# Batch 0's q in rows of nine, the token weight cast and then turned, output rows dealt anew (attention followed by a token and channel MLP, one Trainium2 core)

## The chip, the cores and the metric

The kernel runs on one core of one Trainium2 chip. The core has five engines that run side by side: PE (TensorE, matmuls; its weight loads are listed apart as PEld), DVE (VectorE), ACT (ScalarE), POOL (GpSimd) and SP (SyncE, which here issues nearly all transfers). Sixteen DMA engines move data between the chip's memory and the core's SBUF. The metric is the time of one execution in microseconds of device time. Shown times are medians of several runs; the profile is one execution taken by the hardware profiler.

## What is computed

```python
# attention without softmax, 8 batches x 8 heads, 576 tokens, head width 64
kv  = einsum('bhsd,bhse->bhde', k, v)
out = einsum('bhsd,bhde->bhse', q, kv)
out = out / sqrt(mean(out*out, -1) + 1e-6) * g_norm      # then heads side by side: x[b, s, 512]
# MLP over tokens, then over channels
a1  = alpha1 * x + beta1
tok = einsum('ts,bsd->btd', w_tok, a1)                   # w_tok is 576 x 576
u   = x + lam * tok
a2  = alpha2 * u + beta2
y   = u + lam * (maximum(a2 @ w_ch1, 0) @ w_ch2)         # 512 -> 2048 -> 512
```

Everything comes in and goes out as float32.

## The kernel before, in words

A batch has 576 tokens. The kernel holds them as four chunks of 128 and a tail of 64 (chunk 4); two batches share the tail tiles, one in the lower 64 partitions and one in the upper. For each batch the stages are: k and v come in and `kv_product` (L695) or, for batch 1, L798 and L808 multiply them; q comes in, is split into a high and a low bf16 part (`split_q`, L650), and is turned so that channels lie on partitions, by PE for batch 1 (`qt_dma`, L673) and by transposing DMAs from batch 2 on (L659); q times kv and the norm (`qkv_groups`, L1019, L1102); the token product (`tok_groups`, L1168, L1197); u is turned by transposing DMAs into `a2t` (`ut_groups`, L1307); the first channel product into `ht` (`ch1_groups`, L1328, L1370); the second (`ch2_groups`, L1419), whose result is added to u by DVE (L1429) and stored by one DMA per chunk (L1432), or by two for the shared tail (L1436). The last chunk of the last batch is done in two column parts (L1400, L1406, L1409). Batch b's second channel product is mixed with the preparation of batches b+1 and b+2.

Batch 0 goes a way of its own in float32: `load_first` brings k and v in rows of nine (partition p of a head takes tokens 9p to 9p+8, so that a partition reads 2304 bytes in one piece), two heads above one another. q comes in as 128 partitions of four tokens each (L568) with the last 64 tokens as separate tails (L594), is turned by PE with an identity (`qt_first`, L730, L745) and multiplied in `qkv_first` (L929, L954). The token weight comes in as 128 partitions of four rows each (L1521) and 64 more rows (L1525), into memory that `ht` takes later. `wt_groups` turns it by PE in float32 (L1565, L1588); ACT and DVE copy the results to `wt` as bf16. L1610 makes its column sums, L1242 is batch 0's token product. While PE has nothing to do before the first channel product it runs filler matmuls on zeros (L1750).

Because a partition holds four neighbouring tokens, chunk c holds the tokens 4p + OFF[c] with OFF = (0, 2, 1, 3), and a store writes a chunk with one transfer of 128 rows:

```python
P.op("SP", 0.6, lambda e: e.dma_start(out[b, OFF[c]:512:4, :], x), r=keys, dma_us=0.8)
```

The order is not written out by hand. Each operation is recorded with an engine (or a choice of engines), a cost, what it reads (`r`) and writes (`w`); `Prog.plan` and `Prog.schedule` lay the operations out in time by these costs, by due times and by a table of hand-set shifts of single operations at the end of the kernel, and each engine then runs its own list in that fixed order. All transfers but six small ones go out from SP in its list's order; batch 1's k and v wait for "gate", which the second `kv_product` of batch 0 sets.

Of the kernel before, what the change touches and what calls it, by code (L numbers as in the profile page):

```python
# [6 lines left out]
F32 = mybir.dt.float32  # L7
# [456 lines left out]
def bass_transnormer_attn__then__resmlp_affine_kernel(  # L464
# [15 lines left out]
    with ExitStack() as stack:  # L480
# [18 lines left out]
        qf = sb("qf", [128, NH, 4, DH], F32)  # L499
        qft = sb("qft", [128, NH, DH], F32)  # L500
# [5 lines left out]
        qt32 = qflat[:, 0:2048].rearrange("p (h c t) -> p h c t", h=NH, c=2)  # L506
        qtl32 = qflat[:, 2048:2304].rearrange("p (r t) -> p r t", r=4)
# [11 lines left out]
        a2t = sb("a2t", [128, 4, TP + 16], BF16)  # L519
# [7 lines left out]
        wst2 = hst[0:64, 2304:2880]  # L527

# [38 lines left out]
        def load_main(tile, key, src, b, hs, eng="SP"):  # L567
            P.op(eng, 0.6, lambda e: e.dma_start(  # L568
                tile[:, hs].rearrange("p h c d -> p h (c d)"),
                src[b, hs, 0:512, :].rearrange("h (p c) d -> p h (c d)", c=4)),  # L570
                w=[(key, a) for a in range(hs.start // 4, hs.stop // 4)],
                dma_us=3.7 if hs == ALL[0] else 1.5 if hs.start else 2.0)

        def load_tail(tile, key, src, b, lo, eng="SP"):
            P.op(eng, 0.6, lambda e: e.dma_start(
                tile[lo:lo + 64, :, :], src[b, :, 512:576, :].rearrange("h s d -> s h d")),
                w=[key] + [("qft0", a, y) for a in range(2) for y in range(2) if lo == 0],
                dma_us=0.75)
# [5 lines left out]
        def load_first(a):  # L584
            for key, src, tile in (("kf", k, kf), ("vf", v, vf)):
                P.op("SP", 0.6, lambda e, src=src, tile=tile: e.dma_start(
                    nine(tile, 0, a).rearrange("p x c d -> p x (c d)"),
                    src[0, 4 * a:4 * a + 4].rearrange("(x y) (p c) d -> (y p) x (c d)",
                                                      y=2, c=9)),
                    w=[(key, a)], dma_us=2.0 if a and key == "vf" else 1.4)  # L590

        def load_first_tail(a):
            for y in range(2):
                P.op("SP", 0.45, lambda e, y=y: e.dma_start(  # L594
                    qft[0:64, 4 * a + 2 * y:4 * a + 2 * y + 2, :],
                    q[0, 4 * a + y:4 * a + y + 3:2, 512:576, :].rearrange("h s d -> s h d")),
                    w=[("qft0", a, y)], dma_us=0.2)
# [20 lines left out]
        def load_q(b, hs=ALL[0], tails=True):  # L618
            load_main(qf, "qf", q, b, hs)
            if tails:  # L620
                load_tail(qft, "qft%d" % (b % 2), q, b, 64 * (b % 2))

        PAIRS = ((0, 1), (2, 3), (4,))
        OFF = (0, 2, 1, 3)
# [4 lines left out]
        def split_q(b):  # L629
# [4 lines left out]
            for cs, hs in parts:  # L634
# [4 lines left out]
                if n == 1:  # L639
                    src, hi, lo = qft[rows, hs], hi[:, 0], lo[:, 0]  # L640
                    kin = ["qft%d" % par]
                else:
                    src = qf[:, hs, c0 // 2:c0 // 2 + 3:2, :].rearrange("p h c d -> p c h d")
                    kin = [("qf", a) for a in aa]
# [75 lines left out]
        def qt_first():  # L720

            def pair(a, j):
                t = P.ptile(1)
                h0 = 4 * a + 2 * j

                def f(e):
                    for h in range(2):
                        for c in range(2):
                            o = 256 * h + 128 * c
                            m = e.transpose(t.flat()[:, o:o + 128],  # L730
                                            qf[:, h0 + h, 2 * c:2 * c + 2, :].rearrange(
                                                "p c d -> p (c d)"), ident[:])
                    return m
                P.op("PE", 0.5, f, ins=8, r=["ident", ("qf", a)], w=[t])
                P.op(act_dve(512), 0, lambda e: copy(
                    e, qt32[:, h0:h0 + 2].rearrange("p h c t -> p (h c t)"), t.flat()),
                    r=[t], w=[("q32", 2 * a + j)])

            def tail(a):
# [9 lines left out]
                P.op("PE", 0.14, f, ins=4, r=["ident"] + [("qft0", a, y) for y in range(2)], w=[t])  # L749
                P.op(act_dve(128), 0, lambda e: copy(  # L750
                    e, qtl32[:, 2 * a:2 * a + 2, :],
                    t.flat()[:, 0:128].rearrange("p (r s) -> p r s", r=2)),
                    r=[t], w=[("q32t", a)])
            for a in range(2):
                yield lambda a=a: pair(a, 0)
                yield lambda a=a: pair(a, 1)
                yield lambda a=a: tail(a)
# [85 lines left out]
        def xv(b, cs, lo=0, hi=DM):  # L843
# [6 lines left out]
            return xm[rows, b % 2, cs[0]:cs[0] + len(cs), lo:hi]  # L850

        def rv(b, cs, lo=0, hi=DM):
# [5 lines left out]
            return rt[rows, b % 2, cs[0]:cs[0] + len(cs), lo:hi]  # L858
# [11 lines left out]
        def qkv_first():  # L870
# [48 lines left out]
            def main(a):  # L919
                ts = [P.ptile(1), P.ptile(1)]  # L920

                def f(e, j):
                    for c in range(2):
                        for h in range(2 * j, 2 * j + 2):
                            for sh in range(2):
                                for x in range(2):
                                    kr = slice(64 * x, 64 * x + 64)
                                    o = 256 * c + 64 * h
                                    mm = e.matmul(  # L929
                                        ts[x].flat(slice(64 * sh, 64 * sh + 64))[:, o:o + 64],  # L930
                                        qt32[kr, 4 * a + h, c, 64 * sh:64 * sh + 64],
                                        kv32[kr, a, (h + 2 * x) % 4, :], start=True, stop=True,
# [6 lines left out]
                for x in range(2):  # L939
                    norm(lambda x=x: ts[x].flat().rearrange("p (c h d) -> p c h d", c=2, h=4),  # L940
                         (2 * x, 2 * x + 1), HALVES[a], ts[x])

            def tail(a):
# [4 lines left out]
                hs = HALVES[a]  # L948

                def f(e):  # L950
                    for j in range(2):
                        for x in range(2):
                            kr = slice(64 * x, 64 * x + 64)
                            mm = e.matmul(t.flat(kr)[:, 64 * j:64 * j + 64],  # L954
                                          qtl32[kr, 2 * a + j, :], kv32[kr, a, j, :],
                                          start=True, stop=True, skip_group_check=True)
                    return mm
                P.op("PE", 0.2, f, ins=16, r=QT + KVD + [("kv32", a, 0), ("q32t", a)], w=[t])
                sqv, smv = sq4[:, sqs, 0:128], small[:, sms, 0:2]
                P.op("ACT", act_us(128), lambda e: e.activation(  # L960
                    sqv, t.flat()[:, 0:128], ACT.Square), r=[t], w=[("sqh", sqs)])
                P.op("DVE", dve_us(128), lambda e: e.tensor_reduce(
                    out=smv, in_=sqv.rearrange("p (h d) -> p h d", h=2), axis=AX.X, op=ALU.add),
# [6 lines left out]
                lo, hi = 256 * a, 256 * a + 256  # L970
                xk, rk = xkeys(0, 4, hs), rkeys(0, 4, hs)
# [821 lines left out]
```

## Time and profile before

| | |
|---|---|
| Median of 3 runs | 356.81 us (356.22 to 357.19) |
| The profiled execution | 356.91 us |
| Its span, first to last instruction | 355.1 us |
| Granted PE clock over the span | 1.000 |
| Read from memory, written to it | 38.82 MB, 9.44 MB |

A profile page gives each engine's busy time as a share of the span, a strip of 40 equal slices with the busy tenths of each, the transfers, and the chain of work that ended last. "PE busy" counts pipelined matmuls, so that a busy PE is not one at its peak. L with a number is a line of the kernel above. In the strip 9 means a busy share of at least 90%; for DMA it is the mean of all 16 DMA engines, so that one engine more loaded than the others doesn't show in it.

### The profile page before, as it was taken

What the parts mean: (1) busy time and instruction counts of PE and PEld (TensorE: products, weight loads), DVE (VectorE), ACT (ScalarE), POOL (GpSimd) and SP (SyncE); (2) the same over time, 40 slices, a digit from 0 to 9 for tenths busy, and PEclk for the clock granted to TensorE, in tenths of its full rate; (3) what the DMA queues carried; (4) which work ended last, traced back from release to release, by engine and by line L of the source; (5) the groups of instructions that cost most, each with busy time, mean ns of one, the idle gap of its engine ahead of it and who ended that gap; (6) DMA issues with size and microseconds to landing.
All of it is one profiled execution on the core that took longest, in us unless ns stands there. A gap on an engine that the chain in (4) does not pass through costs nothing.

```text
span 355.1 us, 7785 instructions
## 1 busy us (share of the span) xinstructions
PE 344.1 (97%) x3501; PEld 198.9 (56%) x3320; DVE 238.7 (67%) x365; ACT 157.0 (44%) x267; POOL 22.2 (6%) x30
## 2 busy tenths in 40 slices
PE   7998999999999999999999999999999999999996
PEld 6776644567554554467644654457744554457643
DVE  3679997874889579968883389945974378830021
ACT  3646961248722585038720386018620285007600
POOL 4161123300000000000000000000000000000000
PEclk9999999999999999999999999999999999999999
DMA  8999999999983599269704496244404010150022
GB/s 280 337 360 372 394 346 362 252 203 248 294 231 78 152 379 154 64 198 346 136 18 133 157 319 133 46 148 64 89 4 146 33 30 2 30 153 11 0 61 89
DMA packets 82761, 60.83 MB, mean 171 GB/s; under 512 B 55773, under 2 KB 66277, under 8 KB 82728
## 3 DMA queue, kind: packets, MB, share of 16 engines
q1 hardware_dynamic: 82704, 60.32, 58.7%
q8 instruction: 27, 0.44, 0.6%
q14 instruction: 6, 0.05, 0.0%
q10 hardware_dynamic: 24, 0.01, 0.0%
HBM read 38.82 MB, written 9.44 MB: 136 GB/s over the span
## 4 chain that ended last, share of the span: by engine, by line
PE 88%; DVE 6%; DMA 3%; issue 1%; SPq 0%
PE ps L1419 30%; PE ps L1370 18%; PE ps L1328 14%; PE ps L1168 7%; PE ps L695 4%; PE ps L1019 2%; PE ps L458 2%; PE ps L1197 1%; DMA vf<-in_v_dram 1%; DVE xm L1429 1%; DMA qt<-qs 1%; DVE a2b L1185 1%; DVE xm L1181 1%; PE ps L1400 1%; PE ps L1217 1%
## 5 line engine op out<-in xcount | busy, mean ns | idle before, releaser
L1419 PE MATMUL ps<-w,ht 128*128 128x512 bf16 x537 | 122.5, 379 | 2.3 <-issue 1.4
L1317 ACT ACTIVATE ht<-ps,hb 128x640 bf16<-128x640 f32 (+1 forms) x112 | 83.7, 747 | 48.7 <-PE ps L1370 35.9
L1419 PEld LDWEIGHTS ps<-w,ht 128*128 128x128 bf16 x560 | 53.5, 98 | 63.6 <-issue 2.0
L1370 PE MATMUL ps<-a2t,w 128*128 128x320 bf16 (+1 forms) x512 | 72.2, 299 | 0.4 <-DMA a2t<-a2b 0.4
L1370 PEld LDWEIGHTS ps<-a2t,w 128*128 128x128 bf16 x512 | 49.5, 98 | 21.4 <-DMA a2t<-a2b 0.8
L1328 PE MATMUL ps<-a2t,w 128*128 128x512 bf16 x232 | 52.7, 379 | 1.3 <-issue 0.6
L766 ACT ACTIVATE kvd<-ps 64x128 bf16<-64x128 f32 x24 | 6.5, 271 | 85.4 <-PE ps L695 85.3
L1328 PEld LDWEIGHTS ps<-a2t,w 128*128 128x128 bf16 x240 | 22.6, 98 | 26.5 <-DMA a2t<-a2b 0.4
L1429 DVE TENSOR_TENSOR xm<-ps,xm 128x512 f32<-128x512 f32 x31 | 20.7, 688 | 24.8 <-PE ps L1419 24.5
L1168 PE MATMUL ps<-rt,wt 128*128 128x512 bf16 x106 | 25.2, 379 | 0.4 <-issue 0.2
L1041 DVE TENSOR_REDUCE small<-sq 128x16 f32<-128x1024 f32 x14 | 16.8, 1214 | 12.9 <-ACT sq L1039 12.7
L1181 DVE TENSOR_TENSOR xm<-ps,xm 128x1024 f32<-128x1024 f32 x14 | 17.1, 1222 | 8.0 <-PE ps L1217 5.1
L695 PEld LDWEIGHTS ps<-vf,kf 64*64 64x64 f32 x1008 | 16.0, 135 | 6.3 <-issue 4.5
L564 ACT ACTIVATE qs<-qf 128x1024 bf16<-128x1024 f32 x13 | 13.4, 1049 | 13.5 <-DMA qf<-in_q_dram 10.7
L1185 DVE TENSOR_TENSOR a2b<-xm,a_bc 128x512 bf16<-128x512 f32 x28 | 18.7, 709 | 0.5
L771 DVE TENSOR_TENSOR kvd<-ps,kvd 64x128 bf16<-64x128 f32 x24 | 6.9, 288 | 18.0 <-ACT kvd L766 17.6
L695 PE MATMUL ps<-vf,kf 64*64 64x64 f32 x1008 | 17.9, 221 | 0.6 <-DMA vf<-in_v_dram 0.6
L1168 PEld LDWEIGHTS ps<-rt,wt 128*128 128x128 bf16 x112 | 10.9, 98 | 12.9 <-issue 0.4
L650 DVE TENSOR_TENSOR qs<-qf,qs 128x1024 bf16<-128x1024 f32 x14 | 16.9, 1217 | 1.5 <-ACT qs L564 1.5
L1060 DVE TENSOR_TENSOR xm<-ps,small 128x1024 f32<-128x1024 f32 x14 | 17.1, 1221 | 0.4
L1429 DVE TENSOR_TENSOR xtl<-ps,xtl 128x512 f32<-128x512 f32 x4 | 2.8, 692 | 20.2 <-PE ps L1419 20.1
L1019 PEld LDWEIGHTS ps<-kvd,qt 128*128 128x128 bf16 x224 | 13.9, 98 | 2.5 <-DMA qt<-qs 0.6
(146 smaller groups left out, 327.9 us busy)
## 6 DMA issues: line engine op xcount, KB each, us to landing
out_dram<-xm SPq DMA_DIRECT2D x31, 256.0 KB, 2.5
qf<-in_q_dram SPq DMA_DIRECT2D x7, 1024.0 KB, 11.4
kf<-in_k_dram SPq DMA_DIRECT2D x6, 1152.0 KB, 7.4
vf<-in_v_dram SPq DMA_DIRECT2D x6, 1152.0 KB, 8.5
stg<-in_moe_w_ch_dram SPq DMA_DIRECT2D x3, 1024.0 KB, 14.1
kf<-in_moe_w_ch_dram SPq DMA_DIRECT2D x2, 1024.0 KB
kf<-in_k_dram SPq DMA_DIRECT2D x2, 576.0 KB, 4.8
vf<-in_v_dram SPq DMA_DIRECT2D x2, 576.0 KB, 5.6
```

The source lines that it names most:

```text
L650: lambda e, hi=hi, lo=lo, src=src: e.tensor_tensor(out=lo, in0=src, in1=hi, op=ALU.subtract), r=kin + kh, w=kl, port=True)
L695: m = e.matmul(t.ap(slice(64 * x, 64 * x + 64))[:, y, 0:64], nine(kf, b, a)[r, x, c, :], nine(vf, b, a)[r, x, c, :], start=(c == 0), stop= ...
L1019: e.matmul(o, w, kvd[:, h, 0, :], start=True, stop=False)
L1060: P.op("DVE", dve_us(64 * m), lambda e: e.tensor_tensor(out=x3, in0=split(raw()), in1=inv, op=ALU.mult), r=[t, ("sm", sms)], w=xk, pri=-200)
L1168: m = e.matmul(t.ap()[:, i, :], tok_w(sc, c), rsrc(b, sc), start=(sc == 0), stop=(sc == 4))
L1181: P.op("DVE", dve_us(512 * n), lambda e: e.tensor_tensor(out=x, in0=t.ap(rows) if n > 1 else t.flat(rows), in1=x, op=ALU.add), r=[t] + xk, ...
L1185: P.op("DVE", dve_sb(512), lambda e, c=c: e.tensor_tensor(out=a2b[rows, c, :], in0=xv(b, (c,)), in1=a2_bc[rows, :], op=ALU.mult), r=xkeys( ...
L1317: o = P.op("ACT", act_us(n) + 0.07 * (b > 0), lambda e: e.activation(dst, src(), ACT.Relu, bias=hb[:, fj:fj + 1]) if b else e.activation(d ...
L1328: m = e.matmul(t.flat(), w, a2t[:, dj, 0:512], start=(dj == 0), stop=(dj == 3))
L1370: m = e.matmul(t.ap()[:, i, 0:n], w1[:, dj, 128 * fj:128 * fj + 128], a2t[:, dj, 320 * i:320 * i + n], start=(dj == 0), stop=(dj == 3))
L1419: m = e.matmul(t.flat(), ht[:, fj, 128 * c:128 * c + 128], w2[:, fj, :], start=(fj == 0), stop=(fj == 15))
L1429: P.op("DVE", dve_us(512), lambda e: e.tensor_tensor(out=x, in0=t.flat(), in1=x, op=ALU.add), r=[t] + keys, w=keys)
```

## The change

Four parts. Batch 0's q is loaded like k and v, two transfers of 512 KB in rows of nine without tails. So that the chunks agree for all batches, chunk c now holds the tokens 9p+c and 9p+c+4 for p from 0 to 63, and the tail holds the tokens 9p+8; q of the later batches is loaded as two transfers for 64 partitions each plus the tail, the token weight as four transfers for 64 partitions each plus the tail, and the stores write rows of that order. The token weight is cast to bf16 first (five casts into memory that `w1` takes later) and turned by matmuls with a bf16 identity in pieces of 64 columns. The table of shifts is a new one. `a2t` is 48 columns wider.

```diff
-        a2t = sb("a2t", [128, 4, TP + 16], BF16)
+        a2t = sb("a2t", [128, 4, TP + 64], BF16)
...
+        wflat = w1[:].rearrange("p j f -> p (j f)")
+        wb = wflat[:, 0:2304].rearrange("p (c s) -> p c s", c=4)
+        wb2 = wflat[0:64, 2304:2880]
...
+        def rows_at(ap, lo, n):
+
+            return ap.rearrange("(p c) f -> p c f", c=9)[:, lo:lo + n, :]
...
+        def load_q0(a):
+            P.op("SP", 0.6, lambda e: e.dma_start(
+                q9[:, 2 * a:2 * a + 2].rearrange("p z c d -> p z (c d)"),
+                q[0, 4 * a:4 * a + 4].rearrange("(z y) (p c) d -> (y p) z (c d)", y=2, c=9)),
+                w=[("qf", a)], dma_us=1.4)
+
+        def load_q(b):
+            v = q[b].rearrange("h (p c) d -> p h c d", c=9)
+            for u in range(2):
+                P.op("SP", 0.6, lambda e, u=u: e.dma_start(
+                    qf[64 * u:64 * u + 64].rearrange("p h c d -> p h (c d)"),
+                    v[:, :, 4 * u:4 * u + 4, :].rearrange("p h c d -> p h (c d)")),
+                    w=[("qf", 0), ("qf", 1)] if u == 0 else ["qfu"], dma_us=1.85)
...
+        def rows_of9(ap, c):
+
+            return ap.rearrange("(p c) f -> c p f", c=9)[c:c + 5:4]
...
-                    for pr in range(2):
-                        h = 4 * a + 2 * pr
-                        m = e.transpose(t.flat()[:, 64 * pr:64 * pr + 64],
-                                        qft[0:64, h:h + 2, :].rearrange("p h d -> p (h d)"),
-                                        ident[0:64, 0:64])
+                    for a in range(2):
+                        for z in range(2):
+                            m = e.matmul(t.flat(slice(64 * z, 64 * z + 64))[
+                                :, 128 * a:128 * a + 128], q9[:, 2 * a + z, 8, :], ident[:],
+                                start=True, stop=True, skip_group_check=True)
...
-                        out[b, OFF[c]:512:4, cols], x[:, cols]), r=keys, dma_us=0.6 if n > 128 else 0.3)
+                        rows_of9(out[b], c)[:, :, cols], x[:, cols]), r=keys, dma_us=0.6 if n > 128 else 0.3)
...
-                    P.op("SP", 0.6, lambda e: e.dma_start(out[b, OFF[c]:512:4, :], x), r=keys,
+                    P.op("SP", 0.6, lambda e: e.dma_start(rows_of9(out[b], c), x), r=keys,
                          dma_us=0.8)
                 else:
                     for i in range(2):
                         P.op("SP", 0.6, lambda e, i=i: e.dma_start(
-                            out[b - 1 + i, 512:576, :], x[64 * i:64 * i + 64, :]),
+                            out[b - 1 + i, 8:S:9, :], x[64 * i:64 * i + 64, :]),
                             r=xkeys(b - 1 + i, c), dma_us=0.4)
...
+            for u in range(2):
+                P.op("SP", 0.6, lambda e, u=u: e.dma_start(
+                    wst[64 * u:64 * u + 64, 2 * i:2 * i + 2, :],
+                    rows_at(moe_w_tok, 4 * u + 2 * i, 2)),
+                    w=[("wst", i)] if u == 0 else [("wsu", i)], dma_us=0.8)
+
+        for what, i in (('k', 0), ('v', 0), ('q', 0), ('k', 1), ('v', 1), ('q', 1), ('w', 0), ('w', 1), ('w', 2)):
...
+            w = wb[:, tc, :] if tc < 4 else wb2
+            return [w[:, x:S:9] for x in ((sc, sc + 4) if sc < 4 else (8,))]
...
+            def cast(m):
+                src, dst = (wst[:, m, :], wb[:, m, :]) if m < 4 else (wst2, wb2)
+                P.op(act_dve(576, 1.7), 0, lambda e: copy(e, dst, src),
+                     r=[("wst", m // 2), ("wsu", m // 2)] if m < 4 else ["wst2"], w=[("wb", m)], port=True)
...
                         for x in range(2):
                             o = 256 * y + 128 * x
-                            m = e.transpose(t.flat(slice(0, n))[:, o:o + 128],
-                                            wrow(i + 2 * x, s0 + y), ident[:])
+                            for z, ap in enumerate(wrow(2 * i + x, s0 + y)):
+                                m = e.matmul(t.flat(slice(64 * z, 64 * z + 64))[:, o:o + 128],
+                                             ap, identb[:], start=True, stop=True,
+                                             skip_group_check=True)
```

The turning of the token weight is then 32 such matmuls in four groups, four for the last 64 columns and nine for its tail rows, 45 in all, where there were 25 transposes. The norm of batch 0's tail is done once for all eight heads instead of once for each half. The split of q (`split_q`) and the loops of `qkv_first` follow the new order of the chunks.

More of the change, by code (lines that the diff above doesn't have):

```diff
@@ L756, in qt_first @@
                 yield lambda a=a: pair(a, 1)
-                yield lambda a=a: tail(a)
+            yield tail
         def kv_nine(b):
@@ L1579, in both @@
+            yield last
             def both():
@@ L1684, in mark @@
                 due[o] = 78
+        for i in range(4):
+            for m in range(5):
+                P.readers.setdefault(("w1p", i, 0), []).extend(P.readers[("wb", m)])
         P.chain = True
@@ L1754, in bass_transnormer_attn__then__resmlp_affine_kernel @@
         P.plan(due, 8, {
[7 rows of a table removed]
-            154: "DVE", 181: "DVE", 182: "POOL", 211: "POOL", 215: "DVE"})
[7 rows of a table added]
+            47: "ACT", 58: "ACT", 88: "POOL", 146: "DVE", 168: "ACT", 211: "POOL"})
         P.synchronize()
```

244 lines of the change are left out of this document (119 added, 125 removed), and 14 rows, old and new, of the table start.

## The prediction

> **What bounds the kernel now.** I read the page first, then the DMA view of single stretches, then the chain and the timeline.
>
> ```profile
> span 355.1 us, 7785 instructions
> ...
> PE 344.1 (97%) x3501; PEld 198.9 (56%) x3320; DVE 238.7 (67%) x365; ACT 157.0 (44%) x267; POOL 22.2 (6%) x30
> ...
> DMA  8999999999983599269704496244404010150022
> ```
>
> PE runs from start to end: only 11 us of the span are without a matmul. So time is gained only where PE's own work gets shorter or where it waits or fills, and lost wherever something makes it wait. The DMA strip says what could: the first eleven slices are full, later ones half. The time outside the span is 356.91 - 355.1 = 1.8 us; the profiled execution lies 0.1 us above the median of 356.81, so sums against it are sums against the median.
>
> **Stores.** A chunk's store had 128 rows as the outer dimension on both sides. Now the memory side is 2 x 64 rows, and the 2 lies outermost; the SBUF side still has 128. What does that do? First the price of a store. One stands alone between 345 and 350 us; the DMA view of that stretch says:
>
> ```profile
> DMA packets 144, 0.26 MB, mean 52 GB/s; under 512 B 16, under 2 KB 16, under 8 KB 144
> ...
> q1 hardware_dynamic: 144, 0.26, 13.6%
> ...
> out_dram<-xm SPq DMA_DIRECT2D x2, 256.0 KB, 2.3
> ```
>
> 128 packets are the rows, and 16 small ones stand beside them: I read these as one closing write from each of 16 engines. The store's work is 0.136 x 5 us x 16 = 10.9 engine-us, 0.68 us when all 16 share it. Now transfers with few rows, the six on ACT's queue (four of one row, two of four rows: twelve rows): the queue's packets, first and last of the six:
>
> ```profile
> q10 hardware_dynamic: 24, 0.01, 0.0%
> ...
> xm<-in_moe_lam_dram ACTq DMA_DIRECT2D x1, 2.0 KB
> ...
> xtl<-in_moe_beta_dram ACTq DMA_DIRECT2D x1, 2.0 KB
> ```
>
> Twelve rows would give 12 + 6 x 16 = 108 packets if every transfer closed on 16 engines. There are 24: one closing write for each row. A transfer is thus dealt to engines along its outer dimension, one engine for one row, four for four. [...] No run of before has a large transfer with so small an outer dimension, so its cost is bounded: 0.68 us if it is spread nevertheless, 10.9 / 2 = 5.4 us on two engines. I take 5.4, as the ACT queue's rows are the nearest.
>
> [...]
>
> **What 5.4 us does at the end.** Timeline of SP, and the page's row of the last store (64 KB, 1.7 us to landing):
>
> ```profile
> 342.60 7.24 SPq L1432 DMA_DIRECT2D out_dram<-xm  x3
> 351.98 0.96 SPq L1409 DMA_DIRECT2D out_dram<-xm  x2
> ```
> ```profile
> out_dram<-xm SPq DMA_DIRECT2D x1, 64.0 KB, 1.7
> ```
>
> The last three chunks' stores are issued from 342.6 on, some 3.5 us apart, then the two parts of the last chunk (192 and 64 KB, by bytes 4.1 and 1.4 us on two engines). They no longer keep up: they queue, and end at 342.6 + 1.6 + 3 x 5.4 + 4.1 + 1.4 = 365.9, where 1.6 is a store's landing time less its transfer (2.3 in the 345 to 350 stretch, less 0.68). Before, the last landed at about 352.6 + 1.7 = 354.3. **Plus 11.6 us**, and no work can hide it, since nothing follows.
>
> **What it does in the body.** DMA view of 72.5 to 232.5 us (first store to the transposes of batch 5's a2t), and of 232.5 to 342.5:
>
> ```profile
> q1 hardware_dynamic: 50880, 28.97, 68.2%
> ...
> qf<-in_q_dram SPq DMA_DIRECT2D x5, 1024.0 KB, 11.4
> ...
> out_dram<-xm SPq DMA_DIRECT2D x16, 256.0 KB, 2.5
> ...
> a2t<-a2b SPq DMA_TRANSPOSE x19, 2.4
> ```
> ```profile
> q1 hardware_dynamic: 12768, 6.29, 22.5%
> ...
> out_dram<-xm SPq DMA_DIRECT2D x12, 256.0 KB, 2.7
> ```
>
> In the first stretch an engine has 0.682 x 160 = 109.1 us of work, 16 x 0.68 = 10.9 of it stores. The two store engines would have 109.1 - 10.9 + 16 x 5.4 = 184.6 us in 160: 24.6 us too much. To this comes the next term.
>
> **Loads in halves.** q of the later batches now goes to 64 partitions at a time. The trace has such transfers: the tail's store is two of 64 rows. DMA view of 339 to 342.5, and then two stretches of the early loads, 13 to 14 (128 partitions) and 15 to 16 us (by SP's order, the token weight's 64 last rows pass about there):
>
> ```profile
> DMA packets 160, 0.26 MB, mean 75 GB/s; under 512 B 32, under 2 KB 32, under 8 KB 160
> ...
> q1 hardware_dynamic: 160, 0.26, 32.3%
> ```
> ```profile
> 13.00:14.00 1.00, 1.00 (x72) 1.00 (x71) 0.97 (x4) 0.71 (x3) 0.00 (x0) 1.00 0.99 392
> ...
> 15.00:16.00 1.00, 0.85 (x6) 0.50 (x5) 0.94 (x4) 1.00 (x3) 0.88 (x1) 1.00 0.96 180
> ```
>
> All 16 engines take part (32 closing writes for two), yet the same 256 KB cost 0.323 x 3.5 x 16 = 18.1 engine-us against 10.9, 1.66 times as much; and from 15 to 16 us the engines are busy (0.96) while only 180 GB/s move instead of 392. So half the partitions take bytes at about half the rate. Bounds for 1 MB of q: 4 x 0.68 = 2.7 us if halves cost nothing, 5.4 at half the rate; I take 1.66 x 2.7 = 4.5, plus 1.8 us for each of five loads, 9 us.
>
> [...]
>
> So the two engines are 24.6 + 9 = 33.6 us behind where batch 5's transposes go out. Timeline of SP and PE:
>
> ```profile
> 225.19 7.33 SPq L1307 DMA_TRANSPOSE a2t<-a2b  x5
> 236.96 2.34 PE L1370 MATMUL ps<-a2t,w 128*128 128x320 bf16 x16
> ```
>
> They left SP by 232.5, landed 2.4 us later, and PE took them at 236.96: 2.1 us of slack. The transposes stand in the same queue behind the stores, so PE would **wait some 31 us** in all up to there, spread over the batches. What else is queued: SP issues in order, so that q, k and v of the next batch and the transposes of q stand behind the stores too, but those have tens of microseconds of slack. After 232.5 an engine has 0.225 x 110 = 24.8 us, the two 24.8 + 12 x 4.7 = 81 in 110: they catch up, and no more is lost before the end. Bounds of this term: 0 (the slack of other stages covers all) to 40.
>
> **The head.** The chain, before the first channel product:
>
> ```profile
> 11.91 1.03 PE ps L1750 x4
> ...
> 15.65 0.54 PE ps L1750 x2
> 16.19 0.95 PE ps L1565 x8
> ...
> 17.52 0.82 PE ps L1565 x6
> 18.34 0.68 PE ps L1588 x5
> 19.02 0.82 PE ps L1565 x6
> ...
> 25.29 2.02 PE ps L798 x64
> ...
> 34.72 1.07 PE ps L673 x16
> ```
>
> The token weight's transposes take 0.95 + 0.82 + 0.68 + 0.82 = 3.27 us of PE. New: 45 products, 128 columns each, at 1.07 / 16 = 67 ns in L673: 3.0 us one after another, half if the two 64-column halves run side by side as in L798 (32 ns for each 64 x 64 pass). Their weights are strided, which costs:
>
> ```profile
> L1565 PEld LDWEIGHTS ps<-ident,ht x20: 108/208/212, 15.8 to 19.4; 128*128 128x128 f32 x16, 128*64 128x64 f32 x4
> L730 PEld LDWEIGHTS ps<-ident,qf x16: 137/140/142, 8.2 to 14.8; 128*128 128x128 f32 x16
> ```
>
> 208 ns strided against 140; half of 208 for 64 columns, and none hidden, gives 45 x 0.104 = 4.7 us. So between -1.8 and +1.4 us; I take -1.4, since L1565 itself took 119 ns each in spite of its 208. The five casts (576 columns) stand on DVE or ACT; the nearest rows are casts of 1024, below them two stretches of the windows view:
>
> ```profile
> 27.80 0.68 DVE L565 CAST w<-ht 128x1024 bf16<-128x1024 f32 x1
> ```
> ```profile
> 29.57 1.06 ACT L564 ACTIVATE w<-ht 128x1024 bf16<-128x1024 f32 x1
> ```
> ```profile
> 15.00:20.00 5.00, 4.85 (x53) 3.96 (x55) 3.77 (x13) 3.67 (x11) 2.94 (x4) 1.00 1.04 296
> ...
> 45.00:50.00 5.00, 4.95 (x24) 2.19 (x24) 4.82 (x8) 4.15 (x8) 2.00 (x1) 1.00 1.04 366
> ```
>
> so 0.4 or 0.6 us each, 2 to 3 us in all where DVE and ACT together have 2.6 us free in five; the first stands on the path: +0.5. Without that cover it would be 3. On the other side the token weight's 1.18 MB come in halves: 3.0 us at 392 GB/s become 5.0 (times 1.66), bounds 0 to +3.5; the DMA engines are full until 50 us, so this delays k and v of batch 1 and all weights after them: **+2.0**. The q tails that go away save four issues on SP and as many bytes come in larger pieces; it helps k and v of the second half, where PE fills for 1.03 us: -0.4. Turning q costs PE what it did (the tail's products pass twice in float32). The norm of the tail, done once instead of twice, frees some DVE and ACT. Sum of the head: -1.4 + 0.5 + 2.0 - 0.4 = +0.7, from -3 to +4. DVE is 96% busy from 45 to 50 us, so that a gain on PE ahead of this does not come through whole. The new table of shifts can't put right what it doesn't model; I price it at nothing, within 1 us either way. The wider `a2t` moves addresses only: nothing, for lack of a row that says otherwise.
>
> **Sum.** 356.8 + 11.6 + 31 + 0.7 = **400 us**. In this case the range is 367 (the end alone, with the best head) to 412.
>
> **Rivals.**
> *Stores spread after all, the head gains.* If the two-part side is dealt over 16 engines like 128 rows, nothing is lost behind the head; halves that overlap take the +2.0 away: 356.8 - 1.4 + 0.5 - 0.4 - 0.4 (DVE) = 355.1. For it: only a four-row transfer shows the dealing, and that one had no more than four rows to deal. Faster.
> *Stores spread, halves eat it.* The head's sum then stands alone: 356.8 + 0.7 to + 4, say 359; it decides as soon as halves cost over 1.3 us. The 15 to 16 us row speaks for it.
> *Nothing moves.* Token weight and DMA are later by what PE saves: 356.8.
> *Only the end pays.* Two engines, but the slack of the body takes all: 356.8 + 11.6 = 368; it lies in the first case's range.
>
> **How the numbers follow.** Two engines: 0.62. Spread and faster: 0.20. Spread and about equal: 0.08. Spread and slower: 0.10. This kernel's measurement tells 0.3% (1.1 us) from no change. So faster 0.20, same 0.08, slower 0.72. The range must reach from the spread cases to the two engines: 354.6 to 412, leaving half of the faster case below and little above.
>
> **What would show it.** Right: landing of the xm stores far above 2.5 us; the lone store's 16 closing writes become two; a2t's landing grows from 2.4 us and PE waits on it at L1328 and L1370; ten or more microseconds between the last DVE add and the end. Wrong: 16 closing writes and 2.5 us. For the head: L1565's group near 1.9 us, GB/s near 200 while the token weight and q land, casts between 14 and 20 us. If the stores are spread, the time is 355 to 359 and my main term is nothing.

## The result, and the profile after

The changed kernel took 463.31 us (median of four runs), the kernel before 356.97 beside it: 1.297 times as long, interval 1.289 to 1.304. Forecast were 400 us, within 354.6 to 412. The sign and the main cause held, the size did not: 106 us instead of 43. One of the four runs (500.89 us), with the granted clock lowered throughout (0.73), is left out of the ratio, and since the first profile fell on that run, the profile below is of a repetition (median 461.89 us, the profiled execution 460.99).

The page of the repetition: span, busy times, and the strips of the granted clock and of the transfers.

```profile
span 459.2 us, 7860 instructions
...
PE 366.2 (80%) x3532; PEld 207.7 (45%) x3350; DVE 239.6 (52%) x363; ACT 158.2 (34%) x265; POOL 22.0 (5%) x29
...
PEclk9999999899997999885899958998789989999995
DMA  8999999956093939557058871295405720021111
```

PE was busy 97% of the span before and is now busy 80%. Its clock strip, all nines before, has gaps. The transfer strip ends in four ones, a busy share of one to two tenths: two of sixteen engines are 0.125, and PE has nothing to do in the last of these slices.

Where do 459.2 - 355.1 = 104.1 us come from? The windows view in stretches of 40 us, first of the kernel before (80 to 352 us), then of the changed one (80 to 440), columns as in the prediction:

```profile
sum 272.00, PE 268.60 PEld 149.91 DVE 175.76 ACT 115.95 POOL 0.00; mean PE 38.37 PEld 21.41 DVE 25.11 ACT 16.57 POOL 0.00
```
```profile
200.00:240.00 40.00, 25.95 (x154) 14.23 (x155) 22.68 (x30) 11.73 (x17) 0.00 (x0) 0.83 0.48 129
240.00:280.00 40.00, 22.53 (x291) 11.74 (x262) 11.24 (x19) 8.71 (x16) 0.00 (x0) 0.79 0.73 138
...
sum 360.00, PE 289.60 PEld 158.08 DVE 177.07 ACT 118.23 POOL 0.00; mean PE 32.18 PEld 17.56 DVE 19.67 ACT 13.14 POOL 0.00
```

In the body PE stood still for 272 - 268.6 = 3.4 us; now for 360 - 289.6 = 70.4: 67.0 more. By the same reckoning of the rest, PE stands 2.9 us more ahead of 80 us and 12.1 us more at the end, and it is busy 366.2 - 344.1 = 22.1 us longer. That is the whole difference: **67.0 + 2.9 + 12.1 + 22.1 = 104.1**.

What PE waits for, in the view of waits (who waits, for whom: us in all, times, longest):

```profile
PE ps L1377 <- ACT ht L1324: 17.4, 2, 13.8
PE ps L1335 <- ACT ht L1324: 15.7, 2, 15.5
PE ps L1335 <- DMA a2t<-a2b: 8.9, 1, 8.9
PE ps L1026 <- DMA qt<-qs: 8.3, 2, 5.5
...
PE ps L1377 <- DMA a2t<-a2b: 3.6, 1, 3.6
```

(L1335 and L1377 are L1328 and L1370 of before, L1324 is the relu into `ht`.) The prediction looked for a2t. It is there with 12.5 us, but 33.1 us are waits on ACT, an engine that is busy for only a third of the span. For some 14 us more of PE's standing the profile names no releaser ("issue"). Why is ACT late? The chain from 196 us on:

```profile
196.55 3.63 SPq L618
...
200.22 2.44 SPq L618
...
202.70 13.01 DMA qall<-in_q_dram
...
215.73 0.03 ACT qs L569
...
216.37 0.80 ACT ht L1324
...
217.22 10.92 PE ps L1377 x64
```

and ACT's timeline there (in brackets the idle time before, and its releaser):

```profile
215.73 0.63 ACT L569 ACTIVATE qs<-qall 64x512 bf16<-64x512 f32 x1 [14.79 <-DMA qall<-in_q_dram]
216.37 0.79 ACT L1324 ACTIVATE ht<-ps,hb 128x640 bf16<-128x640 f32 x1
```

SP issues a later batch's q from 196.6 on, two halves and the tail. The tail, issued at 202.7, lands 13.0 us later. ACT works its list in order, and the cast of this tail (64x512) stands at the head: for 14.8 us ACT does nothing. The relu, for which PE waits, stands behind the cast and runs as soon as that is done. The other two long waits on a relu (15.5 and 3.6 us) end in the same way, behind a tail's cast for which ACT had stood 17.8 and 3.9 us.

### The profile page after: what moved, and what is told of

It reads as the page before. It is cut to its first block, busy times and chain, and to the rows that moved or that the text cites. A ratio compares the mean times of both kernels' runs of the same rounds, so it can differ in the third digit from the quotient of the medians.

```text
span 499.1 us, 7902 instructions
## 1 busy us (share of the span) xinstructions
PE 455.3 (91%) x3574; PEld 232.0 (46%) x3350; DVE 239.4 (48%) x363; ACT 160.0 (32%) x265; POOL 22.0 (4%) x29
## 2 busy tenths in 40 slices
DMA packets 81355, 60.82 MB, mean 122 GB/s; under 512 B 54879, under 2 KB 64359, under 8 KB 81322
## 4 chain that ended last, share of the span: by engine, by line
PE 76%; DMA 12%; SPq 7%; ACT 1%; issue 1%; DVE 1%
PE ps L1426 30%; PE ps L1335 13%; DMA qall<-in_q_dram 12%; PE ps L1377 11%; PE ps L1175 7%; SPq L618 3%; PE ps L704 3%; SPq L668 3%; PE ps L1204 1%; PE ps L1249 1%; PE ps L1787 1%; PE ps L1407 1%; PE ps L1224 1%; ACT ht L1324 1%; SPq L1439 1%
## 5 line engine op out<-in xcount | busy, mean ns | idle before, releaser
L1426 PE MATMUL ps<-w,ht 128*128 128x512 bf16 x560 | 164.1, 462 | 1.1 <-ACT ht L1324 0.7
L1324 ACT ACTIVATE ht<-ps,hb 128x640 bf16<-128x640 f32 (+1 forms) x112 | 83.6, 748 | 92.4 <-PE ps L1377 57.7
L1377 PE MATMUL ps<-a2t,w 128*128 128x320 bf16 (+1 forms) x512 | 96.2, 361 | 15.4 <-ACT ht L1324 15.4
L1426 PEld LDWEIGHTS ps<-w,ht 128*128 128x128 bf16 x560 | 61.1, 112 | 93.0 <-issue 88.3
L1335 PE MATMUL ps<-a2t,w 128*128 128x512 bf16 x240 | 72.8, 472 | 13.2 <-ACT ht L1324 9.9
L1377 PEld LDWEIGHTS ps<-a2t,w 128*128 128x128 bf16 x512 | 57.4, 113 | 51.8 <-ACT ht L1324 16.2
L1335 PEld LDWEIGHTS ps<-a2t,w 128*128 128x128 bf16 x240 | 26.5, 114 | 51.5 <-issue 36.6
L1175 PE MATMUL ps<-rt,wt 128*128 128x512 bf16 x112 | 33.6, 459 | 0.0
L569 ACT ACTIVATE qs<-qall 128x1024 bf16<-128x1024 f32 (+1 forms) x21 | 18.6, 907 | 34.0 <-DMA qall<-in_q_dram 34.0
L659 DVE TENSOR_TENSOR qs<-qall,qs 128x1024 bf16<-128x1024 f32 (+1 forms) x20 | 20.7, 1057 | 14.9 <-ACT qs L569 14.8
L704 PE MATMUL ps<-vf,kf 64*64 64x64 f32 x1008 | 21.4, 247 | 0.0
L1026 PEld LDWEIGHTS ps<-kvd,qt 128*128 128x128 bf16 x224 | 16.8, 105 | 4.9 <-issue 2.6
L1026 PE MATMUL ps<-kvd,qt 128*128 128x64 bf16 x224 | 17.4, 205 | 0.8 <-DMA qt<-qs 0.7
## 6 DMA issues: line engine op xcount, KB each, us to landing
qall<-in_q_dram SPq DMA_DIRECT2D x14, 512.0 KB, 12.8
```

The lines of the kernel that those rows point to most:

```text
L569: return e.activation(out, in_, ACT.Identity)
L659: lambda e, hi=hi, lo=lo, src=src: e.tensor_tensor(out=lo, in0=src, in1=hi, op=ALU.subtract), r=kin + kh, w=kl, port=True)
L704: m = e.matmul(t.ap(slice(64 * x, 64 * x + 64))[:, y, 0:64], nine(kf, b, a)[r, x, c, :], nine(vf, b, a)[r, x, c, :], start=(c == 0), stop= ...
L1026: e.matmul(o, w, kvd[:, h, 0, :], start=True, stop=False)
L1175: m = e.matmul(t.ap()[:, i, :], tok_w(sc, c), rsrc(b, sc), start=(sc == 0), stop=(sc == 4))
L1324: o = P.op("ACT", act_us(n) + 0.07 * (b > 0), lambda e: e.activation(dst, src(), ACT.Relu, bias=hb[:, fj:fj + 1]) if b else e.activation(d ...
```

## The experiments

All ratios are against the kernel before run on the same chip, with 95% intervals.

**The changed kernel again.** No edit.

> The changed kernel once more, for a profile and the granted clock. Both theories: 461 to 465 us. Two engines: each 256 KB store closes with 2 writes, and the small packets (4 bytes, one for each engine that took part) fall by 14 for each of 33 xm stores, 462 in all, against before. The clock alone: 463 us would have to come from PE's matmuls being longer by the clock's shortfall; at the 0.905 of the runs shown that is 344.1 / 0.905 - 344.1 = 36 us of the 106.

461.89 us, 1.296 (1.291 to 1.300). The result stands, and this trace was used above.

**Stores as two transfers of 64 rows.** The two parts of the last chunk are split likewise. Nothing else moves: the other four engines have the same lists.

```diff
-                    P.op("SP", 0.6, lambda e: e.dma_start(rows_of9(out[b], c), x), r=keys,
-                         dma_us=0.8)
+                    for u in range(2):
+                        P.op("SP", 0.6 * (1 - u), lambda e, u=u: e.dma_start(
+                            out[b, c + 4 * u:S:9, :], x[64 * u:64 * u + 64, :]), r=keys,
+                            dma_us=0.8 * (1 - u), extra=u > 0)
```

> The changed kernel, with each chunk's store as two transfers of 64 rows (rows 9p+c, then 9p+c+4), whose outer dimension is 64; every other engine's list is the same. Two engines: nearly all of the loss goes, 355 to 364 us, and what is left is the head and the halves. Halves, new order or clock as the cause: the loss stays, above 430 us. Price of a store: two halves of 128 KB, 18.1 engine-us as for the shared tail, so 1.1 us, against 5.4.

373.06 us, 1.043 (1.038 to 1.049): **88.8 of the 105.4 us are gone**. The 355 to 364 us that were expected are missed by 9; "What is left" below comes back to them. Its page has each half of a store landing after 2.4 us (a whole one before: 2.5), and a granted clock with one gap:

```profile
PEclk9999999999999999999699999999999999999999
...
out_dram<-xm SPq DMA_DIRECT2D x62, 128.0 KB, 2.4
```

**The outermost count of a store, in the kernel before.** One edit, U being 2, 4, 8 or 16. The rows are dealt differently, so that the output's rows stand elsewhere; a store is still one transfer of 128 rows of 2 KB.

```diff
-                    P.op("SP", 0.6, lambda e: e.dma_start(out[b, OFF[c]:512:4, :], x), r=keys,
+                    P.op("SP", 0.6, lambda e: e.dma_start(dealt(out[b], c), x), r=keys,
+        def dealt(ap, c):
+            return ap[0:512].rearrange("(p u c) f -> c u p f", u=U, c=4)[c]
```

> The kernel before, with nothing of the change but the shape of its stores: chunk c goes to the rows 8p+4u+c, u outermost, 2 x 64 rows (so the output rows lie elsewhere than the reference's). Two engines: the loss appears here too, 430 to 470 us, as in the changed kernel. Any other cause: 357 us.

> The same edit with 16 outermost: rows 64p+4u+c, 16 x 8 rows (output rows elsewhere again). The memory side cannot be merged into 128 rows here either, but 16 engines divide it. Two engines: 357 us, within 0.3% of before. If it is the shape that doesn't merge, or the scattered rows, and not the count of 2: as slow as the run with 2.

> The kernel before with its chunk stores' rows dealt so that four is the outermost count on the memory's side (rows 16p + 4u + c, u of 4 outermost, p of 32); the output's rows stand elsewhere. Theory (a store is shared out by its outermost count, and the loss follows the time that work stands behind it): a store keeps four engines 2.7 us instead of two 5.4, and 0.7 on sixteen: (2.7 - 0.7) / (5.4 - 0.7) of the 58.5 us is 25 us at most, and less where slack covers it: 364 to 384 us. Rival (two engines are a case of their own, as two lists of descriptors that take turns): 356 to 360 us.

> The same with eight outermost (rows 32p + 4u + c, p of 16): eight engines, 1.35 us each: (1.35 - 0.7) / 4.7 of 58.5 us is 8 us at most: 357 to 365 us by the theory, 356 to 358 by the rival.

| outermost count | us | ratio (interval) | more than before |
|---|---|---|---|
| 2 | 414.99 | 1.163 (1.160 to 1.166) | 58.5 |
| 4 | 374.94 | 1.051 (1.048 to 1.054) | 18.8 |
| 8 | 363.41 | 1.021 (1.017 to 1.024) | 7.3 |
| 16 | 357.53 | 1.003 (1.001 to 1.005) | 1.1 |

With 2, the 430 to 470 us expected were missed by 15; the other three came out as expected. The shape of the store alone costs a kernel in which nothing else is changed 58.5 us. Rows that lie apart are not the reason, since sixteen parts cost 1.1. The loss falls as the count rises; two is no case of its own. The closing writes, read as in the prediction as one from each engine, say how many engines take part. The packets of the whole execution, first of before, then with two outermost:

```profile
DMA packets 82761, 60.83 MB, mean 171 GB/s; under 512 B 55773, under 2 KB 66277, under 8 KB 82728
```
```profile
DMA packets 82299, 60.82 MB, mean 147 GB/s; under 512 B 55311, under 2 KB 65815, under 8 KB 82266
```

The small packets are 462 fewer, 14 for each of the 33 chunk stores (31 whole ones and two parts): 2 closing writes instead of 16. With 4, 8 and 16 there are 55377, 55509 and 55774 of them (the pages of these runs), which to within one packet is what 4, 8 and 16 closing writes a store give. In the changed kernel 462 fewer than before were expected and 894 fewer came (54879), as q is loaded otherwise too; against the same kernel with split stores (55869) they are 990 fewer, 33 x (2 x 16 - 2). So at 2, 4, 8 and 16 a store, whose SBUF side has 128 rows each time, closes with as many writes as the outermost count on the memory's side; for two the prediction had no row.

And the price: the changed kernel's transfers between 446 and 455 us, when only stores run:

```profile
DMA packets 248, 0.46 MB, mean 51 GB/s; under 512 B 4, under 2 KB 86, under 8 KB 248
...
q1 hardware_dynamic: 248, 0.46, 13.2%
```

13.2% of 16 engines are 2.1 engines; 0.262 MB at 51 GB/s are 5.1 us a store. The prediction took 5.4.

By what way does the slow store reach PE in the kernel before, whose order is untouched? The waits of the run with two outermost:

```profile
DVE xm L1064 <- DMA out_dram<-xm: 23.8, 4, 12.8
...
PE ps L1374 <- DVE xm L1064: 17.9, 3, 11.7
...
PE ps L1023 <- DMA qt<-qs: 13.6, 1, 13.6
```

The step of the norm that writes `xm` (L1064) waits until stores that still read this memory are done, and PE waits for DVE. The other large wait is on q's transposes. None of PE's waits there is on a2t. Before, DVE never waits on a store; in the changed kernel it does so for 12.6 us.

**The last batch's stores alone split.** The edit of the second run for the last batch only.

> The changed kernel with the chunk stores of the last batch alone as two transfers of 64 rows each; those of batches 0 to 6 stay as they are. Theory (the end costs what the prediction put it at, and the rest of the 89 us lies in the body): 461.9 - 11.6 = 450 us, within 447 to 453; the last add of VectorE and the end of the span then stand 3 to 5 us apart. Rival (the backlog of the body's stores is what the end waits for): under 445 us, or over 456.

450.55 us, 1.264 (1.260 to 1.267): 11.3 us gained, as expected. The last add, in DVE's timeline of this run, where the span is 449.0 us:

```profile
445.02 0.29 DVE L1418 TENSOR_TENSOR xm<-ps,xm 128x128 f32<-128x128 f32 x1 [0.34 <-PE ps L1412]
```

and in the changed kernel, where the span is 459.2:

```profile
444.25 0.29 DVE L1413 TENSOR_TENSOR xm<-ps,xm 128x128 f32<-128x128 f32 x1 [0.34 <-PE ps L1407]
```

From add to end 3.7 us instead of 14.7. So of the 88.8 us, 11.3 stand behind PE's last product and 77.5 in the body.

**The order without hand-set shifts.** The table at the end of the kernel is emptied, with the few choices of engine that stand beside it, in the kernel with split stores, in the changed kernel and in the kernel before.

```diff
-        P.plan(due, 8, {
-            36: 9.74, 53: 6.5, 54: 20.77, 56: 10.25, 57: 5.48, 62: 5.5, 63: 7.2, 68: 18.5,
...
+        P.plan(due, 8, {}, {})
```

> The changed kernel with split stores, and with an empty table of shifts, so that the planner's own order runs: q of batch b+2 is then issued ahead of the transposes of that stage, as in the kernel before, and not behind them and the stores. Theory (the new order puts q's loads late, so that ACT stands waiting for them with the relu of PE's results behind): 357 to 362 us, PE's waits on ACT's ht near nothing. Rival (what is left of the loss after the split, 16.6 us, is the head and loads in halves): 370 to 375 us, as with the table.

> The changed kernel with its stores as they are (2 x 64 rows) and with an empty table. If two causes add up, stores on two engines and the order: near the 415 us of the kernel before with such stores, 405 to 425. If the stores alone make it, whatever the order: 455 to 465.

> The kernel before with an empty table, to know what a table is worth by itself: 356.5 to 361 us by both theories; if a table is worth as much as 15 us, 370.

| | with its table | without |
|---|---|---|
| before | 356.3 | 373.09, 1.047 (1.042 to 1.053) |
| split stores | 373.06 | 377.49, 1.059 (1.056 to 1.062) |
| changed | 461.89 | 437.11, 1.226 (1.221 to 1.231) |

I had expected 357 to 362 us of the first, with the new table as what holds the split kernel back. That failed: an empty table is no neutral one, since the table of before is worth 16.8 us to its kernel. The changed kernel's 437 us lie between the two ranges that were expected (405 to 425, 455 to 465). The pairs are of use still. In the one plain order the two-engine stores cost 437.1 - 377.5 = 59.6 us, as in the order of before (58.5). The new table saves 4.4 us when stores are spread and **loses 24.8 us when they are not**.

**q ahead of the transposes.** SP's list alone is altered: from batch 3 on, q's loads go out as soon as the plan has the casts before them done. Once in the changed kernel, once in that with split stores. (`LIFT` lists these loads.)

```diff
+        for o in P.ops:
+            if o.idx in LIFT:
+                o.start = min(o.start, max(y.end for y in o.deps))
+        P.sequence.sort(key=lambda o: (o.start, o.idx))
         P.synchronize()
```

> The changed kernel, with only SyncE's own order altered: from batch 3 on, q's loads of a stage are issued as soon as the plan has q's casts of the batch before done, ahead of two to four of that stage's qt transposes and of its chunk stores; TensorE, VectorE, ScalarE and GpSimd keep their order. Theory (q's load stands late behind the stores, ScalarE waits on it with the cast at the head of its queue, and the relu stands behind the cast): q is asked for some 14 us sooner (the four qt transposes ahead of it hold SyncE for 14.2 and 16.8 us), the 43.7 us that ScalarE waits on qall in six waits fall below 20, and the time falls to 425 to 450 us. Rival (the qt and a2t transposes, queued behind the stores, are what TensorE waits for): q ahead of the transposes makes them later, and the time stays at 455 to 475 us.

> The same alteration of SyncE's order on the kernel with each chunk store as two transfers of 64 rows (373.1 us). Theory (of the 15.6 us that it keeps over the kernel before, some 11 come after the head, from q's loads that stand behind the transposes: ScalarE waits 12.4 us on qall): 362 to 369 us. Rival (the transposes are then late instead, or the halves take the time): 371 to 378 us.

The changed kernel: 449.89 us, 1.264 (1.261 to 1.266), 12.0 us gained, at the edge of what the theory gave. Its waits:

```profile
PE ps L1026 <- DMA qt<-qs: 33.4, 5, 10.0
PE ps L1335 <- DMA a2t<-a2b: 12.8, 1, 12.8
...
ACT qs L569 <- DMA qall<-in_q_dram: 2.0, 1, 2.0
...
PE ps L1335 <- ACT ht L1324: 1.5, 1, 1.5
```

ACT's wait on q, 43.7 us in the changed kernel, is 2.0; with it go PE's 33.1 us on the relu. That part of the theory is shown. But PE now waits 33.4 us on q's transposes instead of 8.3: the rival's wait takes the place. What stands behind the stores waits for them, and the order only picks which. With split stores the same alteration makes it slower, 387.44 us, 1.090 (1.085 to 1.094), by 14.4, above the ranges of both sides: there q's place in the new order was the better one, and my theory of the rest fell.

**Transfers in halves, in the kernel before.** q of batches 1 to 7, the token weight, the chunk stores, each as two transfers of 64 partitions, same rows, same place in SP's list; then all three. q's edit:

```diff
-                tile[:, hs].rearrange("p h c d -> p h (c d)"),
-                src[b, hs, 0:512, :].rearrange("h (p c) d -> p h (c d)", c=4)),
+                        tile[64 * u:64 * u + 64].rearrange("p h c d -> p h (c d)"),
+                        src[b, :, 256 * u:256 * u + 256, :].rearrange("h (p c) d -> p h (c d)", c=4)),
```

> The kernel before with one thing altered: q of batches 1 to 7 comes as two transfers to 64 partitions each, the same rows in the same places, in the same place of SyncE's queue; all other orders stay. By the 18.1 against 10.9 engine-us per 256 KB of the lone stores it costs 7 x 4 x 7.2 / 16 = 12.6 us of the queue, 1.8 us a batch. Theory (the queue has slack in every stage, and halves alone hardly show): 356 to 359 us. Rival (the halves make the 15.6 us that the kernel with split stores keeps): 362 to 372 us.

> The kernel before with the token weight's two large transfers as four of 64 partitions each, the same rows in the same places; all else stays. The prediction's price: 3.0 us of a full queue become 5.0, so +2.0: 358 to 359 us. Rival (what stands behind it early in the queue has more slack than that, or less): 356 to 357, or over 360 us.

> The kernel before with each chunk store as two transfers of 64 rows each, the same rows in the same places; all else stays. A store costs the 16 engines 1.13 us instead of 0.68. Theory (the queue has slack where stores go, after 72 us, and the end is a few tenths later): 356 to 358 us. Rival (the stores' halves carry half of the 11.6): 360 to 363 us.

> The kernel before with q of batches 1 to 7, the token weight and each chunk store as two transfers of 64 partitions each, the same rows in the same places and the same place in SyncE's queue: the transfers of the changed kernel with split stores, in the order and with the products of the kernel before. Some 12.6 + 2 + 14.8 = 29 us more of the queue. Theory (what the split kernel keeps is its order and its head, not the halves): 357 to 361 us. Rival (the halves): 365 to 373 us.

| in halves | us | ratio (interval) |
|---|---|---|
| q | 361.84 | 1.017 (1.013 to 1.021) |
| token weight | 358.58 | 1.005 (1.003 to 1.008) |
| chunk stores | 360.24 | 1.009 (1.006 to 1.012) |
| all three | 367.85 | 1.033 (1.031 to 1.035) |

Together 11.6 us over before, by parts 5.6, 2.0 and 3.6. The token weight is what the prediction took, 2.0. For q I had expected 356 to 359 us, for the stores 356 to 358, for all three 357 to 361: missed by 3, 2 and 7 us, the last two in favour of the rival. Most of the loss arises early. The token product of batch 2 starts at 110.4 us in the run with all three, against 102.0 before, and every later batch is 9 to 10 us late. In that run the transfer engines are full for most of the time up to 105 us (their share is 0.8 from 85 to 95), and the chain goes through q's loads there. The windows view (the last two columns are the transfer engines' share and GB/s) and the chain:

```profile
95.00:100.00 5.00, 5.00 (x36) 3.30 (x34) 3.76 (x5) 3.25 (x5) 0.00 (x0) 1.00 1.12 242
```
```profile
25.17 11.88 DMA qf<-in_q_dram
...
92.28 6.97 DMA qf<-in_q_dram
```

**Half of the token weight from ACT's queue.** In the split kernel without a table, its upper halves are issued by ACT.

```diff
-                P.op("SP", 0.6, lambda e, u=u: e.dma_start(
+                P.op("SP", 0.6, lambda e, u=u: (nc.scalar if u else e).dma_start(
                     wst[64 * u:64 * u + 64, 2 * i:2 * i + 2, :],
```

> As the first of these, but the upper halves of the token weight are issued from ACT's queue, so that both halves of the partitions fill at the same time; all lists else the same. If 64 partitions take bytes at half the rate: the token weight lands about 2 us earlier, GB/s near 380 instead of 250 to 275 between 10 and 20 us, and the end is 1 to 2 us earlier. If it is the shape or size of the pieces that is slow: no change within 0.3%.

384.34 us, 1.077 (1.071 to 1.083): slower by 6.9 than with SP alone (377.49), which neither side had expected. The chains of the two, SP alone first:

```profile
3.46 11.06 DMA qall<-in_q_dram
```
```profile
3.49 15.27 DMA qall<-in_q_dram
```

The second queue brings the token weight beside q, which is needed first: q lands 4.2 us later. What makes the rest of the 6.9 was not followed.

## Why the forecast was right in kind and wrong in size

**Two engines for a store, 5.4 us each.** Right: 2 closing writes, 5.1 us a store, and 58.5 to 88.8 us for the shape alone, depending on the order that it meets. It was argued from transfers of one and four rows; that the memory's side decides while the SBUF side has 128 rows was the author's estimate, shown by no row of before. The runs with 2, 4, 8 and 16 show it: as many closing writes a store.

**The end, +11.6 us.** Right: 11.3.

**The body, +31 us (0 to 40).** The step that failed: the two engines cost the body 77.5 us. The 31 even held 9 for q's halves, which are not among these 77.5, so that 24.6 less 2.1 of slack, some 22, stand against them. Three statements of the term were wrong, and with them the path on which the loss reaches PE.

First, that q, k, v and q's transposes "have tens of microseconds of slack". That was never worked out from a row, and it is the sentence on which the term rested: only a2t's slack was taken from the timeline. In the trace a2t makes up 12.5 us of PE's waits; q, by way of ACT's list, makes 33.1, and q's transposes 8.3. Moving q ahead took the 33.1 away and raised q's transposes to 33.4, and in the kernel before with such stores a2t makes up nothing. The sign that was looked for, a landing of a2t far above 2.4 us, did not come either (median 2.4 in both kernels), whereas q's halves land after 12.8 us in the changed kernel and 7.0 with split stores. The memory of `xm` that a slow store keeps from DVE was in no term.

Second, that the two engines' excess over a long stretch (24.6 + 9 us in 160) is what PE loses. Right ahead of the q in the chain above SP issues two stores in a row:

```profile
195.44 1.06 SPq L1439 DMA_DIRECT2D out_dram<-xm  x2
```

At 5.1 us each they are some 10 us of work for the two engines (an estimate), and q's tail behind them takes 13.0 us to land, though the mean of all engines is a share of only 0.48 from 200 to 240 us. A mean over 160 us shows neither such a burst nor who stands behind it.

Third, that they "catch up" after batch 5's transposes. The token product's start (timeline of PE, batches 2, 5 and 7), before and changed:

```profile
101.97 1.89 PE L1168 MATMUL ps<-rt,wt 128*128 128x512 bf16 x7
...
219.01 3.19 PE L1168 MATMUL ps<-rt,wt 128*128 128x512 bf16 x13
...
300.75 3.62 PE L1168 MATMUL ps<-rt,wt 128*128 128x512 bf16 x15
```
```profile
117.18 1.03 PE L1175 MATMUL ps<-rt,wt 128*128 128x512 bf16 x4
...
289.86 3.62 PE L1175 MATMUL ps<-rt,wt 128*128 128x512 bf16 x15
...
392.72 3.62 PE L1175 MATMUL ps<-rt,wt 128*128 128x512 bf16 x15
```

15.2 us late, then 70.9, then 92.0: 21 us are lost between batch 5 and batch 7, where next to nothing more was to be lost.

**The table of shifts, priced at nothing.** Wrong beside these stores: it loses 24.8 us against no table. One part of it is shown, q's place (12.0 us). What the rest is was not taken apart.

**PE's own time** was in no term. It is busy 22.1 us longer. 6.8 of these are there with split stores too (350.9 us, clock 0.99); the other 15 come with the gaps: between 80 and 400 us the granted clock of stretches of 40 us is 0.79 to 0.96.

**Halves.** The rate was right in kind: with split stores the stretch from 355 to 372 us, when only stores run in halves of 64 rows, has 1.31 MB at 32.9% of 16 engines, so 0.329 x 17 x 16 = 89.5 engine-us for five times 256 KB, 17.9 each where 18.1 were reckoned; and the token weight's +2.0 measures 2.0. Wrong was that q's halves cost only where the two engines are full: q of batches 1 and 2 falls into the full stretch that the strip of before showed, and all of q's halves cost 5.6 us with no slow store in the kernel.

**The head.** The gain of 1.4 us on PE did not come. PE's groups in the first 60 us by shape, the token weight's products, before and changed:

```profile
L1565 PE MATMUL ps<-ident,ht 128*128 128x128 f32 x16 | 2.4, 283 | 0.0
L1565 PE MATMUL ps<-ident,ht 128*64 128x128 f32 x4 | 0.8, 285 | 0.0
L1588 PE MATMUL ps<-ident,ht 64*128 64x64 f32 x4 | 0.7, 293 | 0.0
L1588 PE MATMUL ps<-ident,ht 64*64 64x64 f32 x1 | 0.2, 216 | 0.0
```
```profile
L1584 PE MATMUL ps<-identb,w 128*64 128x128 bf16 x32 | 2.7, 292 | 0.3 <-DVE xm L915 0.3
L1602 PE MATMUL ps<-identb,w 128*64 128x128 bf16 x4 | 0.6, 282 | 0.0
L1623 PE MATMUL ps<-identb,w 64*64 64x64 bf16 x9 | 0.8, 281 | 0.0
```

4.1 us in either. Twenty-five products in float32 became 45 in bf16, and took as long. The four products of q's tail, now matmuls in float32, stand there as eight records (L752, x8, 0.7 us); before, the four transposes were four (L745, x4, 0.7 us). The head as a whole was put at +0.7 us, from -3 to +4; batch 0's token product starts 4.4 us later (26.54 against 22.15). How much of that reaches the end was not measured.

**What is left.** With split stores the changed kernel stays 16.6 us over before. Transfers in halves cost 11.6 us in the order of before, but that can't simply be taken off: there 8.4 us are lost by batch 2's token product, while the split kernel is 3.7 us late at that of batch 2 and of batch 3, and 12.0 at that of batch 4 (before: 138.14 and 178.21 us). The last two in the split kernel:

```profile
141.86 3.62 PE L1180 MATMUL ps<-rt,wt 128*128 128x512 bf16 x16
...
190.22 3.40 PE L1180 MATMUL ps<-rt,wt 128*128 128x512 bf16 x15
```

Between them ACT waits 4.8 us for q's tail, PE 3.8 us for the relu behind its cast, and the granted clock is 0.80 to 0.86 from 170 to 190 us: the same path as above, in small. How the 16.6 us divide into halves, order and head stays open. No run came out below the kernel before.

## What to carry to other kernels

Before a layout is changed, write down the outermost count on the memory's side of each large transfer that follows from it: 128 rows dealt as 2 x 64 are one instruction as before, and here kept two engines for 5.1 us a store. Where a queue gets slow bursts, ask what waits for the memory that they still read, take the slack of every user behind them from the timeline, and follow each into the engine that waits in order: one late cast, for which ACT stood 14.8 us, held up a relu, and with it PE. A hand-set order that helps beside one kind of store can cost time beside another (4.4 us saved, 24.8 lost): measure a change with its order and without.

## What was not expected of the hardware

The granted clock is low where PE has gaps. With split stores PE is busy 39.0 us in the stretch from 80 to 120 us, at 1.00; in the same kernel with q ahead of the transposes it is busy 34.1 us, at 0.91:

```profile
80.00:120.00 40.00, 34.14 (x263) 20.70 (x230) 24.83 (x42) 19.19 (x31) 0.00 (x0) 0.91 0.60 149
```

So a wait on a transfer seems to cost its own length and something more (PE is busy 22.1 us longer in the changed kernel, 6.8 us with split stores). In the changed kernel's end, where no product runs, the clock is 0.50 (row below), and of the 360 stretches of 1 us from 80 to 440 us, 282 have 1.00, 61 have 0.50 and only 17 something between. That the gaps lower the clock, rather than the clock making gaps, was not tested by itself.

```profile
450.00:455.00 5.00, 0.00 (x0) 0.00 (x0) 0.00 (x0) 0.00 (x0) 0.00 (x0) 0.50 0.13 51
```

In the run with half of the token weight on ACT's queue, the second issuing queue brought no more bandwidth: in the first 30 us 248 GB/s moved on the mean, against 300 with SP alone, and what came later was mixed into what was needed first (q 4.2 us later).
